# First gate products moved into the opening, down products turned, a third PSUM bank

## The chip, the core and the metric

The kernel runs on one core of a Trainium2 chip. The metric is the device time of one execution in microseconds. Five engines have a part in it: TensorE (PE in the rows, its weight loads PEld), VectorE (DVE), ScalarE (ACT), GpSimd (POOL), and SyncE (SP), which here only issues DMAs and waits.

## The reference

A recurrence over 768 steps for 4 batches and 8 heads of width 48, then a gated layer over its 3072 rows of 384 numbers:

```python
for t in range(S):                       # S = 768
    cur = np.einsum('bhd,bhe->bhde', u[None] * kt, vt)
    y[:, :, t] = np.einsum('bhd,bhde->bhe', rt, state + cur)
    state = wt[:, :, :, None] * state + np.einsum('bhd,bhe->bhde', kt, vt)
...
gate = 1.0 / (1.0 + np.exp(-(x @ w_gate)))   # 384 -> 1536
val = x @ w_val                              # 384 -> 1536
return (gate * val @ w_out).astype(np.float32)   # 1536 -> 384
```

The weights come as 64-bit numbers. The kernel unpacks each into a high and a low part of 32 bits, and forms each product of the gated layer from three matmuls: low part by high, high by low, high by high.

## The kernel before, in words

The recurrence is cut into 6 pieces of 128 steps. With 4 batches this makes 24 chunks of attention, q = 0 to 23, of which four (one for each batch) make up a row n = q // 4 of the gated layer, 512 tokens. A chunk q turns its keys (`turn_k`, tile pk), forms scores and sums (`pairs`, `add_up`, tiles pa and pv), mixes (`mix`) and turns its result (`turn_x`, tile px). Each of these tiles is a PSUM bank from `att_bank` (L204), which has two in turn.

The gated layer of a row n runs over 12 slices f of the hidden width. A slice is: `gate` (L480, nine matmuls into bank pg, through `up`), `sigmoid` on ACT, `value` (L487, nine matmuls into bank pu), `hidden` on DVE (the product, L492), `hidden_hi` on ACT (hh, L496), `hidden_lo` on DVE (hl, L500), and `down` (L502), which adds into the banks po0 to po3, one for each 128 tokens: there the tokens' hidden numbers are the stationary operand and 384 columns of the weights move. With the last slice `down` also copies each of the four banks by ACT (L515) into a tile o of a pool with two buffers, and issues its way out from ACT's queue (L517).

PSUM has eight banks: two of `att_bank`, pg, pu, po0 to po3.

The order is written in two ways. The opening (rows n = 0 and 1 of the gated layer in four groups of two batches, the attention's chunks 0 to 11, the unpacking of all weights, and the beginnings of chunks 12 and 13) is put in order by `Plan` (L142): `add` gives each step an engine, a cost, what it comes after, a rank, and the banks or buffers that it takes or gives back; `run` starts on each engine the step of lowest rank that is ready. Behind it comes the late loop (L630), written out by hand: for n from 2 to 5 and twelve slices each, the gate products of a slice, a part of the attention's chunk for row n + 1, the value products, another part, and then the down products of the slice before, which stand in `last`. In the row n = 5 no attention is left. The engines take their instructions in the order in which they are listed.

At the end every engine loads a flag and branches around `general` (L651), a slow way for inputs out of bounds, which does not run here.

Of the kernel before, what the change touches and what calls it, by code (L numbers as in the profile page):

```python
# [44 lines left out]
def general(ctx: ExitStack, tc: tile.TileContext, dec, tok, wts, u, out, whi, wlo, ident):  # L45
# [5 lines left out]
    rows = ctx.enter_context(tc.tile_pool(name="rows", bufs=1, space=bass.MemoryType.DRAM)).tile([B, S, DM], F32, name="rows")  # L51

    def tiles(name, shape, dtype=F32):
        return pool.tile(shape, dtype, name=name)
# [36 lines left out]
    for c in range(NC_):  # L91
        for b in range(B):
            nc.sync.dma_start(d[:, b], dec[b * NC_ + c])
        with tc.For_i(0, C) as i:
            def at(first, step):
                return d[:, :, first:first + NP * step].rearrange("a b (p c) -> a b p c", c=step)[:, :, :, bass.ds(i, 1)].broadcast_to(shape)
            for o in range(2):
                for b in range(B):
                    nc.sync.dma_start(vb[64 * o:64 * o + D, b], values[c, 2, o, bass.ds(i, 1), b].partition_broadcast(D))
            nc.vector.tensor_tensor(out=kv, in0=vb, in1=at(WW, C), op=ALU.mult)  # L100
            nc.vector.tensor_tensor(out=mix, in0=kv, in1=ub, op=ALU.mult)
            nc.vector.tensor_tensor(out=mix, in0=mix, in1=state, op=ALU.add)
            nc.vector.tensor_tensor(out=mix, in0=mix, in1=at(WW + NP * C, C), op=ALU.mult)
            nc.vector.tensor_tensor(out=state, in0=state, in1=at(1, W1), op=ALU.mult)
            nc.vector.tensor_tensor(out=state, in0=state, in1=kv, op=ALU.add)
            for j in range(2):
                nc.tensor.matmul(py[j][:2, :DM], lhsT=heads, rhs=mix[:, 2 * j:2 * j + 2], start=True, stop=True)
                nc.scalar.copy(y[:, 2 * j:2 * j + 2], py[j][:2, :DM].rearrange("a (b p e) -> a b p e", b=2, e=D))
            for b in range(B):
                for o in range(2):  # L110
                    nc.sync.dma_start(
                        rows[b, bass.ds(c * C + i, 1)].rearrange("t (p o e) -> o t p e", o=2, e=D)[o], y[o:o + 1, b])
# [5 lines left out]
    flat = rows.rearrange("b s e -> (b s) e")  # L118
    with tc.For_i(0, NG) as g:
        nc.sync.dma_start(x, flat[bass.ds(g * C, C)])  # L120
        for k in range(NKT):
            nc.tensor.transpose(out=px[:, k * C:(k + 1) * C], in_=x[:, k * P:(k + 1) * P], identity=ident)
        px3 = px[:, :DM].rearrange("a (k c) -> a k c", c=C)
        nc.scalar.copy(xhi, px3)
        nc.vector.tensor_tensor(out=xlo, in0=px3, in1=xhi.bitcast(F32), op=ALU.subtract)
        for f in range(NFF):
            for s, acc in enumerate((pg, pu)):
                for k in range(NKT):
                    cols = slice(s * DM + k * P, s * DM + (k + 1) * P)
                    for j, (w, a) in enumerate(((wlo, xhi), (whi, xlo), (whi, xhi))):  # L130
                        nc.tensor.matmul(acc[:, :C], lhsT=w[f][:, cols], rhs=a[:, k], start=k == 0 and j == 0, stop=k == NKT - 1 and j == 2)
            nc.scalar.activation(gate, pg[:, :C], AF.Sigmoid)
# [3 lines left out]
            for j, (a, w) in enumerate(((hl, whi), (hh, wlo), (hh, whi))):  # L136
                nc.tensor.matmul(po[:, :DM], lhsT=a, rhs=w[f][:, 2 * DM:], start=f == 0 and j == 0, stop=f == NFF - 1 and j == 2)
        nc.scalar.copy(x, po[:, :DM])
        nc.sync.dma_start(out[bass.ds(g * C, C)], x)


class Plan:  # L142
# [49 lines left out]
def tile_kernel(ctx: ExitStack, tc: tile.TileContext, dec: bass.AP, tok: bass.AP, wts: bass.AP, u: bass.AP, out: bass.AP):  # L192
# [5 lines left out]
    p2 = own.enter_context(tc.tile_pool(name="p2", bufs=2))  # L198
    ps1 = own.enter_context(tc.tile_pool(name="ps1", bufs=1, space=PSUM))
    att2 = own.enter_context(tc.tile_pool(name="att2", bufs=2, space=PSUM))  # L200
    early = tc.tile_pool(name="early", bufs=4)
    stage = early.__enter__()

    def att_bank(name):  # L204
        return att2.tile([P, 512], F32, tag="att", name=name)

    ident = const.tile([P, P], F32, name="ident")
# [33 lines left out]
        return raws[f].bitcast(dtype).rearrange("a (c w) -> a c w", w=2)[:, :, i]  # L241

    def w_guard(f):
        sq = p1.tile([P, 3 * DM], F32, tag="sq", name=f"sq{f}")
        nc.scalar.activation(sq, word(f, 1, F32), AF.Square, accum_out=acc_s[:, f:f + 1])
        nc.scalar.activation(sq, sq, AF.Relu, bias=1.0, scale=-1.0 / TINY ** 2, accum_out=acc_t[:, f:f + 1])

# [24 lines left out]
    def place(q):  # L272
        return q % B * NC_ + q // B
# [228 lines left out]
    def down(n, f, i0, i1):  # L502
        hh, hl = hid["hi", n, f, i0], hid["lo", n, f, i0]
        for i in range(i0, i1):
            if f == 0:
                po[n, i] = ps1.tile([P, 512], F32, tag=f"po{i}", name=f"po{n}_{i}")
            c = slice((i - i0) * C, (i - i0 + 1) * C)
            for j, (h, w) in enumerate(((hl, whi), (hh, wlo), (hh, whi))):
                nc.tensor.matmul(  # L509
                    po[n, i][:, :DM], lhsT=h[:, c], rhs=w[f][:, 2 * DM:],  # L510
                    start=f == 0 and j == 0, stop=f == NFF - 1 and j == 2,
                )
            if f == NFF - 1:
                o = p2.tile([P, DM], F32, tag="o", name=f"o{n}_{i}")
                nc.scalar.copy(o, po[n, i][:, :DM])  # L515
                g = place(n * B + i)
                nc.scalar.dma_start(out[g * C:(g + 1) * C, :], o)  # L517

    def check_bounds():
        nc.vector.tensor_scalar(out=fine[:L, 0], in0=acc_d, scalar1=2.0 ** 90, scalar2=None, op0=ALU.is_le)  # L520
# [14 lines left out]
    def add(name, engine, cost, after, rank, f=None, *args, take=(), give=()):  # L535
        plan.add(name, engine, cost, after, rank, f and (lambda: f(*args)), take, give)
# [46 lines left out]
    for g, (n, i0, i1) in enumerate(GROUPS):  # L583
        m = i1 - i0
        for f in range(NFF):
            a, name = (n, f, i0, i1), f"{g}_{f}"
            k = 100 + f + LAGS[g]
            soon = k / 1000 - 1
            up_cost = 9 * (0.008 + 0.056 * m)
            need = [f"xl{n * B + i}" for i in range(i0, i1)] + [f"wl{f}", f and f"pu{g}_{f - 1}"]  # L590
            add("pg" + name, "PE", up_cost, need, k, gate, *a, take=["pg", "unit"] + [f"po{i}" for i in range(i0, i1) if f == 0])
            add("sg" + name, "ACT", 0.14 + 0.13 * m, ["pg" + name], soon, sigmoid, *a, give=["pg"])
            add("pu" + name, "PE", up_cost, ["pg" + name], k, value, *a, take=["pu"])
            add("hm" + name, "DVE", 0.15 + 0.135 * m, ["pu" + name, "sg" + name], soon, hidden, *a, give=["pu"])
# [12 lines left out]
    def steps(q):  # L607

# [75 lines left out]
```

## Time and profile before

| what | us |
|---|---|
| median of three runs | 605.04 (603.53 to 608.01) |
| profiled execution, its own time | 603.9 |
| its span, from the first to the last instruction | 602.2 |
| PE busy | 558.7 |
| DVE busy | 332.6 |
| ACT busy | 201.6 |
| POOL busy | 96.7 |

The time of an execution is that of the device; the span is what the profiler saw of it, 1.7 us less. Busy times overlap, so they say which engine is full, and not where the time goes. In a timeline the first column is the start in us from the span's start, the second the duration; matmuls follow each other faster than they last, so that the pace of a run of matmuls is read from the starts of two groups. A matmul's end is modelled. A bracket at the end of a row is the idle time ahead of it and what ended it.

### The profile page before, as it was taken

The page shows a single profiled execution, that of the slowest core. Times are in us where ns is not written, and L with a number is a line of the kernel's source. Part 1 is how long each engine was busy: PE and PEld are TensorE (multiplying, and loading weights), DVE is VectorE, ACT ScalarE, POOL GpSimd, SP SyncE. Part 2 cuts the span into 40 slices and gives each one's busy share as a digit, 9 for nine tenths or more (in the row PEclk, how much of TensorE's full clock was granted, in tenths as well). Part 3 has the DMA queues.
Part 4 walks back from the last instruction along what each step waited for, and adds up shares of the span by engine and source line. Part 5 has one row for each costly group of instructions (what it writes and reads, how often), then busy time and mean ns, then how long its engine had stood idle before and what let it go on. Part 6 is the DMA issues. An engine that isn't in the chain of part 4 may idle for free. (4 is left out here: it accounts for less than half of the span.)

```text
span 602.2 us, 14593 instructions
## 1 busy us (share of the span) xinstructions
PE 558.7 (93%) x6474; PEld 498.4 (83%) x6474; DVE 332.6 (55%) x570; ACT 201.6 (33%) x402; POOL 96.7 (16%) x86
## 2 busy tenths in 40 slices
PE   4475899999999999899999999999999999999994
PEld 3365799999999999788888888888888888888883
DVE  4989879989685653254554554554454453221220
ACT  3648683444333322312222322222321221222212
POOL 3352111102120502002201211211211210000000
PEclk9999699999999999999999999999999999999997
DMA  8788920033233130122033033022033000100001
GB/s 250 250 327 290 347 95 1 1 87 83 72 121 126 50 125 3 53 86 86 3 87 87 28 112 86 2 86 87 35 106 87 1 1 2 54 1 0 1 1 57
DMA packets 12055, 50.85 MB, mean 84 GB/s; under 512 B 1376, under 2 KB 4576, under 8 KB 10448
## 3 DMA queue, kind: packets, MB, share of 16 engines
q1 hardware_dynamic: 8528, 45.11, 23.4%
q10 hardware_dynamic: 3456, 4.72, 2.2%
q8 instruction: 53, 0.87, 0.6%
q14 instruction: 18, 0.15, 0.1%
HBM read 45.11 MB, written 4.72 MB: 83 GB/s over the span
## 5 line engine op out<-in xcount | busy, mean ns | idle before, releaser
L474 PE MATMUL pg<-x,w 128*128 128x256 f32 (+1 forms) x864 | 171.6, 344 | 2.1 <-DVE w L267 2.1
L474 PE MATMUL pu<-x,w 128*128 128x256 f32 (+1 forms) x864 | 170.5, 342 | 0.0
L474 PEld LDWEIGHTS pg<-x,w 128*128 128x128 f32 x864 | 138.3, 193 | 17.8 <-DVE w L267 2.2
L474 PEld LDWEIGHTS pu<-x,w 128*128 128x128 f32 x864 | 136.2, 191 | 17.3
L509 PE MATMUL po<-w,hh 128*128 128x384 f32 x576 | 147.7, 337 | 0.0
L492 DVE TENSOR_TENSOR sg<-pu,sg 128x256 f32<-128x256 f32 (+1 forms) x96 | 53.4, 557 | 149.9 <-PE pu L474 148.9
L509 PE MATMUL po<-w,hl 128*128 128x384 f32 x288 | 101.2, 351 | 7.1 <-DVE hl L500 7.0
L496 ACT CAST hh<-sg 128x256 fp32r<-128x256 f32 (+1 forms) x96 | 49.2, 512 | 170.0 <-DVE sg L492 169.6
L509 PEld LDWEIGHTS po<-w,hh 128*128 128x128 f32 x576 | 105.0, 189 | 0.9
L485 ACT ACTIVATE sg<-pg 128x256 f32<-128x256 f32 (+1 forms) x96 | 46.9, 488 | 141.7 <-PE pg L474 140.1
L314 POOL TENSOR_TENSOR bon<-tok,a 128x384 f32<-128x384 f32 x24 | 35.0, 1457 | 282.7 <-DVE a L310 282.7
L500 DVE TENSOR_TENSOR hl<-sg,hh 128x256 fp32r<-128x256 f32 (+1 forms) x96 | 55.7, 580 | 39.0 <-ACT hh L496 39.0
L509 PEld LDWEIGHTS po<-w,hl 128*128 128x128 f32 x288 | 54.3, 189 | 10.4 <-DVE hl L500 8.4
L303 POOL TENSOR_TENSOR bon<-tok,ub 128x384 f32<-128x384 f32 x24 | 32.6, 1358 | 113.4 <-DMA tok<-tok 61.1
L448 DVE TENSOR_TENSOR bon<-pa,bon 128x192 f32<-128x192 f32 x48 | 15.6, 353 | 49.3 <-PE pa L441 49.2
L348 ACT ACTIVATE junk<-eg 112x1032 bf16<-112x1032 f32 x24 | 25.6, 1066 | 30.7 <-DVE eg L338 30.6
L321 DVE TENSOR_TENSOR_SCAN eg<-pin,ends 112x516 f32<-112x516 f32 x24 | 30.0, 1251 | 4.9 <-DMA pin<-dec 4.9
L338 DVE TENSOR_TENSOR_SCAN eg<-pin,heads 112x516 f32<-112x516 f32 x24 | 30.5, 1270 | 0.0
L353 PE MATMUL pk<-ident,pin 112*128 112x112 f32 x96 | 14.7, 278 | 14.1 <-DVE pin L327 10.2
L306 POOL TENSOR_TENSOR bon<-bon,tok 128x384 f32<-128x384 f32 x24 | 27.3, 1136 | 1.7
L441 PE MATMUL pa<-tok,at 64*32 64x48 f32 x1536 | 23.8, 213 | 2.3 <-DVE at L402 2.3
L353 PEld LDWEIGHTS pk<-ident,pin 112*128 112x128 f32 x96 | 11.5, 150 | 17.1 <-issue 9.0
(62 smaller groups left out, 433.8 us busy)
## 6 DMA issues: line engine op xcount, KB each, us to landing
pin<-dec SPq DMA_DIRECT2D x23, 675.5 KB, 5.8
tok<-tok SPq DMA_DIRECT2D x24, 576.0 KB, 5.8
wraw<-wts SPq DMA_DIRECT2D x12, 1152.0 KB, 12.3
y<-o ACTq DMA_DIRECT2D x24, 192.0 KB, 1.9
pin<-dec SPq DMA_DIRECT2D x1, 448.0 KB, 4.3
pin<-dec SPq DMA_DIRECT2D x1, 227.5 KB, 2.9
ub<-u SPq DMA_DIRECT2D x1, 192.0 KB, 6.7
```

Source lines behind the costliest of these rows:

```text
L303: nc.gpsimd.tensor_tensor(out=bon[q], in0=tk[q][:, 0:DM], in1=ub, op=ALU.mult)
L306: nc.gpsimd.tensor_tensor(out=bon[q], in0=bon[q], in1=tk[q][:, DM:2 * DM], op=ALU.mult)
L314: nc.gpsimd.tensor_tensor(out=by_head(bon[q]), in0=by_head(tk[q][:, 2 * DM:]), in1=a0, op=ALU.mult)
L321: nc.vector.tensor_tensor_scan(out=e[:, 516:0:-1], data0=t[:, 516:0:-1], data1=ends[:, 516:0:-1], initial=0.0, op0=ALU.mult, op1=ALU.add,)
L338: nc.vector.tensor_tensor_scan(out=e[:, WW:WW + 516], data0=t[:, 0:516], data1=heads[:, 0:516], initial=0.0, op0=ALU.mult, op1=ALU.add,)
L353: nc.tensor.transpose(out=t[:, p * L:(p + 1) * L], in_=kk(q)[:, p], identity=ident[:L, :L])
L474: nc.tensor.matmul(t, lhsT=w[f][:, cols], rhs=x[n][:, a, k, i0 * C:i1 * C], start=k == 0 and j == 0, stop=k == NKT - 1 and j == 2)
L485: nc.scalar.activation(sg, hid["g", n, f, i0], AF.Sigmoid)
L492: nc.vector.tensor_tensor(out=sg, in0=hid["u", n, f, i0], in1=sg, op=ALU.mult)
L496: nc.scalar.copy(hh, hid["s", n, f, i0])
L500: nc.vector.tensor_tensor(out=hl, in0=hid["s", n, f, i0], in1=hid["hi", n, f, i0].bitcast(F32), op=ALU.subtract)
L509: nc.tensor.matmul(po[n, i][:, :DM], lhsT=h[:, c], rhs=w[f][:, 2 * DM:], start=f == 0 and j == 0, stop=f == NFF - 1 and j == 2,)
```

## The change

Five things change. The lines of the changed kernel stand some 20 to 43 lines further down than those of the kernel before.

The nine gate products of the late loop's first slice (n = 2, f = 0) become a step of the opening's plan, with the highest rank number, after the gate products of the last two groups; the late loop leaves them out.

For n from 2 to 5 `down_turned` takes the place of `down`: the weights are the stationary operand, and all 512 tokens' hidden numbers move, so that each of three banks po0 to po2 holds 128 outputs of 512 tokens. Each bank is copied into a buffer of its own; in the last row the second block is copied by DVE and sent by SyncE. The output is written turned for these rows, in blocks, and the host turns it back.

The bank po3, which these rows do not need, is the third one of `att_bank` in the late loop.

The tile sq, which receives the squares of the weights' guard, is bf16 instead of fp32. `general` writes the same blocks; it is written out for each block of rows instead of looping.

```diff
     def att_bank(name):
+
+        turns.append(name)
+        if late and len(turns) % 3 == 0:
+            return ps1.tile([P, 512], F32, tag="po3", name=name)
         return att2.tile([P, 512], F32, tag="att", name=name)
...
-        sq = p1.tile([P, 3 * DM], F32, tag="sq", name=f"sq{f}")
+        sq = p1.tile([P, 3 * DM], BF16, tag="sq", name=f"sq{f}")
...
                 nc.scalar.copy(o, po[n, i][:, :DM])
-                g = place(n * B + i)
-                nc.scalar.dma_start(out[g * C:(g + 1) * C, :], o)
+                nc.scalar.dma_start(out[n].rearrange("(b c e) -> b c e", b=B, c=C)[i], o)
+
+    def down_turned(n, f, i0, i1):
+
+        hh, hl = hid["hi", n, f, i0], hid["lo", n, f, i0]
+        for k in range(NKT):
+            if f == 0:
+                po[n, k] = ps1.tile([P, 512], F32, tag=f"po{k}", name=f"po{n}_{k}")
+            cols = slice(2 * DM + k * P, 2 * DM + (k + 1) * P)
+            for j, (h, w) in enumerate(((hl, whi), (hh, wlo), (hh, whi))):
+                nc.tensor.matmul(po[n, k], lhsT=w[f][:, cols], rhs=h, start=f == 0 and j == 0, stop=f == NFF - 1 and j == 2)
+            if f == NFF - 1:
+                o = p1.tile([P, B * C], F32, tag=f"ot{k}", name=f"o{n}_{k}")
+                y = po[n, k]
+                by_vector = n == NC_ - 1 and k == 1
+                if by_vector:
+                    nc.vector.tensor_copy(out=o, in_=y)
+                else:
+                    nc.scalar.copy(o, y)
+                to = out[n].rearrange("(k p t) -> k p t", p=P, t=B * C)[k]
+                (nc.sync if by_vector else nc.scalar).dma_start(to, o)
...
+    ahead = (2, 0, 0, B)
+    add("ahead", "PE", 2.1, [f"xl{2 * B + i}" for i in range(B)] + ["pg2_11", "pg3_11"], 200, gate, *ahead, take=["pg"])
...
     plan.run()
     early.__exit__(None, None, None)
     stage = own.enter_context(tc.tile_pool(name="late", bufs=2))
+    late = True
...
                 a = (n, 3 * j + i, 0, B)
-                gate(*a)
+                if a != ahead:
+                    gate(*a)
                 sigmoid(*a)
...
                 if last:
-                    down(*last.pop())
+                    down_turned(*last.pop())
...
-    down(*last.pop())
+    down_turned(*last.pop())
```

Where the opening ends, PE had the last group's value products (pu_2_11, slice 11 of the group that starts at the third batch), its down products into po_2 and po_3, and then the late loop's first gate products (pg_0_0):

```order
L474 MATMUL pu_2_11_3325<-x_1106,w_1682 128x256 x9
L509 MATMUL po_2_2326<-w_1682,hl_2_11_3338 128x384
L509 MATMUL po_2_2326<-w_1682,hh_2_11_3336 128x384 x2
L509 MATMUL po_3_2330<-w_1682,hl_2_11_3338 128x384
L509 MATMUL po_3_2330<-w_1682,hh_2_11_3336 128x384 x2
L474 MATMUL pg_0_0_3356<-x_2412,w_236 128x512 x9
L353 MATMUL pk_3368<-ident,pin_2819 128x112 x4
L474 MATMUL pu_0_0_3375<-x_2412,w_236 128x512 x9
```

In the changed kernel the same place on PE reads:

```order
L494 MATMUL pu_2_11_3325<-x_1106,w_1682 128x256 x9
L494 MATMUL pg_0_0_3335<-x_2412,w_236 128x512 x9
L529 MATMUL po_2_2326<-w_1682,hl_2_11_3348 128x384
L529 MATMUL po_2_2326<-w_1682,hh_2_11_3346 128x384 x2
L529 MATMUL po_3_2330<-w_1682,hl_2_11_3348 128x384
L529 MATMUL po_3_2330<-w_1682,hh_2_11_3346 128x384 x2
L373 MATMUL pk_3368<-ident,pin_2819 128x112 x4
L494 MATMUL pu_0_0_3375<-x_2412,w_236 128x512 x9
```

The gate products have moved ahead of the six down products, and nothing else here has moved.

At the program's end, ACT had the last hh, four copies of the banks po_0 to po_3 with an issue behind each, and the flag:

```order
L496 CAST hh_0_11_6680<-sg_0_11_6667 128x512
L515 COPY o_0_6699<-po_0_6290 128x384
L517 DMA y<-o_0_6699 128x384
L515 COPY o_1_6705<-po_1_6294 128x384
L517 DMA y<-o_1_6705 128x384
L515 COPY o_2_6711<-po_2_6298 128x384
L517 DMA y<-o_2_6711 128x384
L515 COPY o_3_6717<-po_3_6302 128x384
L517 DMA y<-o_3_6717 128x384
L651 TENSOR_LOAD flag
L651 COMPARE_AND_BRANCH
```

In the changed kernel ACT's end is:

```order
L516 CAST hh_0_11_6529<-sg_0_11_6516 128x512
L554 COPY o_0_6545<-po_0_6170 128x512
L556 DMA y<-o_0_6545 128x512
L554 COPY o_2_6557<-po_2_6178 128x512
L556 DMA y<-o_2_6557 128x512
L694 TENSOR_LOAD flag
L694 COMPARE_AND_BRANCH
```

Two copies and two issues are left on ACT; the block between them has gone to DVE and SyncE. SyncE's end in the changed kernel, behind the last loads of the attention's inputs (pin, tok):

```order
L301 DMA pin_5607<-dec 112x1544
L306 DMA tok_5609<-tok 128x1152
L556 DMA y<-o_1_6551 128x512
L694 TENSOR_LOAD flag
L694 COMPARE_AND_BRANCH
```

Before, the flag's load stood right behind the last load of tok there; now the issue of an output block stands between.

## Rows read from the trace of the kernel before

**Rows 1.** The page: span, and busy time, share of the span and instructions.

```profile
span 602.2 us, 14593 instructions
PE 558.7 (93%) x6474; PEld 498.4 (83%) x6474; DVE 332.6 (55%) x570; ACT 201.6 (33%) x402; POOL 96.7 (16%) x86
```

**Rows 2.** Table of stretches: from:to, length, busy of each engine, PEclk, DMA share, GB/s.

```profile
270.00:330.00 60.00, 60.00 (x738) 51.44 (x738) 29.46 (x53) 15.59 (x31) 12.41 (x9) 1.00 0.22 63
```

**Rows 3.** Waits of PE, 270 us to the end: total, times, longest (us).

```profile
PE total L527 <- DVE count L525: 0.7, 1, 0.7
```

**Rows 4.** Timeline of PE, the end of the opening.

```profile
245.07 1.23 PE L474 MATMUL pu<-x,w 128*128 128x256 f32 x9
247.77 0.44 PE L509 MATMUL po<-w,hl 128*128 128x384 f32 x1 [1.48 <-DVE hl L500]
...
248.95 2.25 PE L474 MATMUL pg<-x,w 128*128 128x512 f32 x9
251.03 0.55 PE L353 MATMUL pk<-ident,pin 112*128 112x112 f32 x4
```

**Rows 5.** Timeline of ACT, the sigmoid of the opening's last gate.

```profile
243.31 0.38 ACT L485 ACTIVATE sg<-pg 128x256 f32<-128x256 f32 x1
```

**Rows 6.** Timeline of PE, the late loop: its first value products, and slices of the last row.

```profile
251.35 2.30 PE L474 MATMUL pu<-x,w 128*128 128x512 f32 x9
253.59 0.69 PE L370 MATMUL pa<-pin 48*64 48x64 f32 x32
...
537.26 2.20 PE L474 MATMUL pu<-x,w 128*128 128x512 f32 x9
539.30 0.33 PE L509 MATMUL po<-w,hl 128*128 128x384 f32 x1
...
541.41 2.24 PE L474 MATMUL pg<-x,w 128*128 128x512 f32 x9
```

**Rows 7.** Timeline of ACT, the end of the program.

```profile
592.34 0.48 ACT L515 COPY o<-po 128x384 f32<-128x384 f32 x1 [1.61 <-PE po L509]
592.85 0.34 ACTq L517 DMA_DIRECT2D y<-o  x1
...
593.79 1.03 ACTq L517 DMA_DIRECT2D y<-o  x1
595.92 0.48 ACT L515 COPY o<-po 128x384 f32<-128x384 f32 x1 [2.16 <-SPq L651]
...
597.38 0.64 ACTq L517 DMA_DIRECT2D y<-o  x1
```

**Rows 8.** Timeline of PE, matmuls of the last slice's first and last down products.

```profile
591.79 0.51 PE L509 MATMUL po<-w,hh 128*128 128x384 f32 x2
...
593.35 0.51 PE L509 MATMUL po<-w,hh 128*128 128x384 f32 x2
```

**Rows 9.** The flag's line, L651: duration ns min/median/max, first and last start us.

```profile
L651 SPq EVENT_SEMAPHORE  x8: 17/17/17, 526.4 to 599.7; - x8
L651 SPq TENSOR_LOAD <-flag x1: 572/572/572, 522.9 to 522.9; - x1
...
L651 SPq COMPARE_BRANCH  x1: 45/45/45, 523.6 to 523.6; - x1
...
L651 ACTq COMPARE_BRANCH  x1: 54/54/54, 598.6 to 598.6; - x1
L651 ACTq EVENT_SEMAPHORE  x1: 17/17/17, 601.3 to 601.3; - x1
```

**Rows 10.** Groups by form: count | busy us, mean ns of one | idle before, releasers.

```profile
L492 DVE TENSOR_TENSOR sg<-pu,sg 128x512 f32<-128x512 f32 x48 | 33.2, 692 | 119.9 <-PE pu L474 119.9
...
L485 ACT ACTIVATE sg<-pg 128x512 f32<-128x512 f32 x48 | 28.5, 593 | 104.2 <-PE pg L474 103.4 <-PE pa L380 0.8
L348 ACT ACTIVATE junk<-eg 112x1032 bf16<-112x1032 f32 x24 | 25.6, 1066 | 30.7 <-DVE eg L338 30.6
...
L246 ACT ACTIVATE sq<-sq 128x1152 f32<-128x1152 f32 x12 | 14.0, 1166 | 0.4
```

More of the change, by code (lines that the diff above doesn't have):

```diff
@@ L50, in general @@
     bank = ctx.enter_context(tc.tile_pool(name="banks", bufs=1, space=PSUM))
-    rows = ctx.enter_context(tc.tile_pool(name="rows", bufs=1, space=bass.MemoryType.DRAM)).tile([B, S, DM], F32, name="rows")
+    rows = ctx.enter_context(tc.tile_pool(name="rows", bufs=1, space=bass.MemoryType.DRAM)).tile([NC_, B, C, DM], F32, name="rows")
     def tiles(name, shape, dtype=F32):
@@ L111, in general @@
                     nc.sync.dma_start(
-                        rows[b, bass.ds(c * C + i, 1)].rearrange("t (p o e) -> o t p e", o=2, e=D)[o], y[o:o + 1, b])
+                        rows[c, b, bass.ds(i, 1)].rearrange("t (p o e) -> o t p e", o=2, e=D)[o], y[o:o + 1, b])
     x, px = tiles("x", [P, DM]), bank.tile([P, 512], F32, name="px")
@@ L117, in general, with feed @@
     pg, pu, po = (bank.tile([P, 512], F32, name=n) for n in ("pg", "pu", "po"))
-    flat = rows.rearrange("b s e -> (b s) e")
-    with tc.For_i(0, NG) as g:
-        nc.sync.dma_start(x, flat[bass.ds(g * C, C)])
+    def feed(n, b, turned):
+        nc.sync.dma_start(x, rows[n, b])
         for k in range(NKT):
@@ L135, in general @@
             nc.vector.tensor_tensor(out=hl, in0=h, in1=hh.bitcast(F32), op=ALU.subtract)
-            for j, (a, w) in enumerate(((hl, whi), (hh, wlo), (hh, whi))):
-                nc.tensor.matmul(po[:, :DM], lhsT=a, rhs=w[f][:, 2 * DM:], start=f == 0 and j == 0, stop=f == NFF - 1 and j == 2)
-        nc.scalar.copy(x, po[:, :DM])
-        nc.sync.dma_start(out[bass.ds(g * C, C)], x)
+            for k in range(NKT if turned else 1):
+                cols = slice(2 * DM + k * P, 2 * DM + (k + 1) * P)
+                for j, (a, w) in enumerate(((hl, whi), (hh, wlo), (hh, whi))):
+                    first, done = f == 0 and j == 0 and k == 0, f == NFF - 1 and j == 2
+                    if turned:
+                        nc.tensor.matmul(po[:, k * C:(k + 1) * C], lhsT=w[f][:, cols], rhs=a, start=first, stop=done, skip_group_check=True)
+                    else:
+                        nc.tensor.matmul(po[:, :DM], lhsT=a, rhs=w[f][:, 2 * DM:], start=first, stop=done)
+        nc.scalar.copy(x, po[:, :DM])
+        if turned:
+            to = out[n].rearrange("(k p b c) -> b p k c", p=P, b=B, c=C)[b]
+            nc.sync.dma_start(to, x.rearrange("p (k c) -> p k c", c=C))
+        else:
+            nc.sync.dma_start(out[n].rearrange("(b c e) -> b c e", b=B, c=C)[b], x)
+    for n in range(NC_):
+        for b in range(B):
+            feed(n, b, n >= 2)
 class Plan:
@@ L200, in tile_kernel @@
     att2 = own.enter_context(tc.tile_pool(name="att2", bufs=2, space=PSUM))
+    late = False
     early = tc.tile_pool(name="early", bufs=4)
     stage = early.__enter__()
+    turns = []
     def att_bank(name):
+        turns.append(name)
+        if late and len(turns) % 3 == 0:
+            return ps1.tile([P, 512], F32, tag="po3", name=name)
         return att2.tile([P, 512], F32, tag="att", name=name)
@@ L515, in down @@
                 nc.scalar.copy(o, po[n, i][:, :DM])
-                g = place(n * B + i)
-                nc.scalar.dma_start(out[g * C:(g + 1) * C, :], o)
+                nc.scalar.dma_start(out[n].rearrange("(b c e) -> b c e", b=B, c=C)[i], o)
[4 more added lines that the diff above has]
+                po[n, k] = ps1.tile([P, 512], F32, tag=f"po{k}", name=f"po{n}_{k}")
+            cols = slice(2 * DM + k * P, 2 * DM + (k + 1) * P)
+            for j, (h, w) in enumerate(((hl, whi), (hh, wlo), (hh, whi))):
[6 more added lines that the diff above has]
+                    nc.vector.tensor_copy(out=o, in_=y)
+                else:
+                    nc.scalar.copy(o, y)
+                to = out[n].rearrange("(k p t) -> k p t", p=P, t=B * C)[k]
+                (nc.sync if by_vector else nc.scalar).dma_start(to, o)
     def check_bounds():
@@ L678 @@
     args = [nc.dram_tensor(n, a.shape, mybir.dt.from_np(a.dtype), kind="ExternalInput").ap() for n, a in arrays.items()]
-    args.append(nc.dram_tensor("y", (B * S, DM), F32, kind="ExternalOutput").ap())
+    args.append(nc.dram_tensor("y", (NC_, B * C * DM), F32, kind="ExternalOutput").ap())
     with tile.TileContext(nc) as tc:
@@ L682 @@
     r = run_bass_kernel_spmd(nc, [arrays], core_ids=[0])
-    return r.results[0]["y"]
+    y = r.results[0]["y"]
+    y = np.concatenate([y[:2].reshape(-1, B * C, DM), y[2:].reshape(-1, DM, B * C).transpose(0, 2, 1)])
+    return np.ascontiguousarray(y.reshape(NC_, B, C, DM).transpose(1, 0, 2, 3).reshape(B * S, DM))
```

## The prediction

> **What bounds the kernel now.** I read four views: the page's busy times and the table of stretches (which engine is full, where), the list of TensorE's waits (whom it waits for), then the timeline at the three places that the diff touches, and last the rows of the program's end.
>
> TensorE (PE) is busy for 558.7 of a span of 602.2 us [rows 1]. In the table of stretches the reader is to see 60.00 us busy of 60.00 from 270 to 330, at a granted clock of 1.00, its upper level of 2.4 GHz [rows 2]; the three next stretches up to 510 read alike. From 270 us to the end the list of PE's waits has one row, 0.7 us [rows 3]. So up to about 250 us, while the attention and the unpacking of weights run beside the products, PE sometimes waits; behind that it is the bound, and only fewer or shorter PE instructions, or a shorter end, give time back. A wait taken from ACT, VectorE (DVE) or a queue there is worth nothing.
>
> **The change part by part.** The profiled execution took 603.9 us, span 602.2; the median of the three runs is 605.04. I work out what is saved and take it from all three alike.
>
> *The gate products of the late loop's first chunk, nine matmuls of 512 columns, are listed ahead of the opening's last down products.* Before, PE ends the opening's last value products (issued at 245.07, 1.23 long, so to 246.3), waits 1.48 us for hl of DVE, starts six down products at 247.77, is at the gate products at 248.95 and through their issue at 251.03 [rows 4]. Six down products so cost 1.18 and nine gate products 2.08. Now the gate products start at some 246.2 (the next matmul may be issued about 0.1 before the modelled end of the last) and end at 248.3. By then hl has been there for 0.5 us, so the down products begin at once. Their first matmul no longer stands behind a wait, so they take some 1.05 to 1.1, and PE is at the next work at 249.3 to 249.4 instead of 251.03: **1.7 us**. The gate products' only wait is for ACT's read of their bank, which was at 243.31, 0.38 long [rows 5]. What was late next, ACT's sigmoid of this gate, stays behind the opening's two last output copies, but those come at PE's pace too. Bounds: 1.48, the wait alone, to 1.8.
>
> *Down products of n from 2 to 5 turned.* Each of 48 chunks had 12 matmuls of 384 columns (3 for each of 4 blocks of rows) and now has 9 of 512 (3 for each of 3 blocks of outputs): 4608 columns either way, 1.92 us at 2.4 GHz. The trace has both shapes side by side: in the last stretch, where no attention runs beside, twelve down products from 539.30 to 541.41, 2.11 us; nine value products of the same 512 columns, with a weight slice as the stationary operand as the turned ones have it, from 537.26 to 539.30, 2.04 us [rows 6]. Over the bare columns this is 15.8 ns for each matmul of 384 and 13.3 for each of 512. Three matmuls fewer at 13.3 to 15.8 ns are 0.040 to 0.047 us; the plain difference is 0.07, of which the rest may be due to what DVE and ACT do beside. I take 0.045. It counts in 46 chunks: the last one starts when hl comes, whichever shape is ahead of it, and one chunk is followed by PE's wait for the bounds' count [rows 3], which swallows it. 46 x 0.045 = **2.1 us**. The trace shows no turned product with hl or hh as moving operand, so the bounds are wide: at best 0.07 x 46 = 3.2; at worst the slowest nine products of 512 columns that these rows show, from 251.35 to 253.59, 2.24 us [rows 6], which would be 0.13 x 46 = 6.0 lost. I stay at the value products, whose form is the nearest.
>
> The Trainium skill, "TensorE: Matmul & The Clock Gate", section "Back-to-back issue gap", gives N / 2.4 + 2.5 ns for a warm matmul of N columns; the rows show a fixed part of 13.3 to 15.8 ns, so they do not agree. By the Trainium skill's figure the 138 matmuls fewer (3 x 46) would be worth an estimated 0.35 us in place of 2.1.
>
> *The end.* Before, the program's last four output copies share two buffers. The reader is to see that ACT copies and sends two, and starts the third only at 595.92 after an idle of 2.16 [rows 7], though the last matmul pair, 0.51 long, starts at 593.35 [rows 8]. The row names SyncE as the releaser, but the code has the reason: the third copy takes the first one's buffer, which must have landed. The last issue starts at 597.38, takes 0.64, and 4.2 us later the span ends. In these 4.2 ACT loads the flag, branches at 598.6 and has its next instruction at 601.3 [rows 9]: 2.7 us for nothing but the branch, then 0.9 of closing. Now three blocks have three buffers, and nothing waits for a landing. PE ends at 593.86 as before, since the last hl sets that. ACT's copy started 0.04 behind its last matmul (591.79 + 0.51, then 592.34 [rows 7, 8]), so the last one starts at 593.9. It has 512 columns from PSUM, 0.59 us as the sigmoid of this shape [rows 10]: 594.5. Its issue takes 0.34 to 1.03, as the rows have it [rows 7], so it ends at 594.9 to 595.5; and 4.2 us more give 599.1 to 599.7, 2.5 to 3.1 less than 602.2. A second path is new: the block that DVE copies (0.69 [rows 10], to about 593.9) goes out by SyncE, which before had branched at 523.6 and now issues at 594.0, 0.3 long, loads the flag (0.57), branches and stands for 2.8 us (523.6 to 526.4 [rows 9]): 597.7. I allow 1 us for its eight waits [rows 9] and what follows them, which before lay beside ACT's branch, and the closing 0.9: 599.6. So I take **2.7 us**, bounds 1.0 to 3.2.
>
> The Trainium skill, "Runtime: NRT & Kernel Launch", section "Instruction fetch mechanics", says that a taken branch to a page that is not loaded must fetch it first. The 2.7 and 2.8 us agree, and it is a reason to expect them once more on each engine that now branches late.
>
> *What costs or gives nothing.* The third bank for the attention's chunks: it can only take waits away, and PE has none behind 270 us [rows 3]; where the attention's results come from ACT or DVE, one or two products of over 2 us lie between. Cover gone, a bank's wait would be one copy, 0.6 us. The guard's squares in bf16: ACT took 1166 ns for 1152 fp32 outputs and 1066 for 1032 bf16 outputs [rows 10], 1.01 and 1.03 ns each, so the type hardly matters to ACT; 0.02 ns more for 1152 outputs in 24 passes would be 0.55 us, the bound either way, and it would mostly lie beside DVE's work on the same weights. Outputs in blocks: the same bytes, three issues instead of four, 0.6 us of copy instead of 0.48, on an ACT that mostly waits for PE.
>
> Sum: 1.7 + 2.1 + 2.7 = 6.5 us. Span 602.2 to 595.7, profiled execution 603.9 to 597.4, median 605.04 to **598.5**.
>
> **Rivals.**
>
> *The end moves less.* SyncE's and DVE's late branches, each with its own fetch, and two transfers of 256 KB that land together, take the place of the removed buffer wait. For it: ACT's issues took 0.64 and 1.03 where others took 0.34 [rows 7], so the end is crowded already. Against it: the 2.16 us of idle are really gone. With 1.0 instead of 2.7: 600.2.
>
> *Columns alone count.* If the 0.07 comes not from the number of matmuls but from what lies beside them, the turned products take the 2.11 of the others, and turning gives nothing: 1.7 + 2.7 = 4.4, 600.6. For it: the two shapes stand in other parts of a chunk, with other work of DVE and ACT beside them. Against it: the rows are from chunks without any attention beside them [rows 6], and the difference is there. By the Trainium skill's 2.5 ns (the page and section above) it would be an estimated 600.3, and the rows do not bear that figure out.
>
> *More than I take.* Turned products at the full pace of the value products, 3.2, and the end at 3.1: 1.7 + 3.2 + 3.1 = 8.0, 597.0.
>
> *Slower.* The turned product is no value product: its moving operand was written by DVE and ACT one chunk ago, and the other buffers of the same pool are written meanwhile. If its nine take 2.24 us, 6.0 are lost against 4.4 won at both ends: 606.6. It decides from 2.11 + 4.4 / 46 = 2.21 us for nine, 245 ns each; slower by over 1% needs some 260 ns each. For it only the slow nine behind the transposes [rows 6]; against it every other nine.
>
> *The change does not do what it says*: the gate moved but held by something I do not see. Then 1.7 is missing, 600.2; I count it within my own case's range.
>
> **How the numbers follow.** My case 0.64, 597.0 to 600.2; the end moves less 0.12; columns alone 0.10; more than I take 0.09; slower 0.05. About 1% is what a measurement of this kernel can tell from no change; for faster that is 599.0 or less. Of my case some two thirds lie there (0.42), with all of the fourth and a little of the others: faster 0.52. Slower by over 1% is left for the turned products alone, 0.03; the rest is 0.45. The range takes in the two cases near 600.4 with the spread of the runs (603.5 to 608.0): 596.3 to 602.5.
>
> **What would show it.** Right: no wait of 1.48 before the opening's last down products, and the gate products right behind the value products; the turned nine at 2.04 to 2.08 us, each chunk 0.04 to 0.05 shorter; the last output copy 0.04 behind the last matmul, and the span's end 5.2 to 5.9 us behind that copy's start. Wrong: turned products over 235 ns apart, new waits of PE behind 250 us, or SyncE's branch as the last thing before the closing by over 1 us.

## The result and the profile after

The changed kernel took 596.59 us (median of four, 595.38 to 597.80), the kernel before 605.28 in the same comparison: a ratio of 0.9853, 95% interval [0.9826, 0.988], so 1.5% faster where 1.1% was forecast. Six further times gave 597.35 against 605.16, ratio 0.986 [0.9837, 0.9883]. The profiled execution took 595.38 against 603.9, with this span and these busy times on its page [rows 1]:

```profile
span 593.7 us, 14287 instructions
PE 555.1 (93%) x6330; PEld 478.6 (81%) x6330; DVE 332.6 (56%) x571; ACT 200.2 (34%) x397; POOL 96.4 (16%) x86
```

The instruction counts fall by 144 matmuls and 144 weight loads, three for each of 48 slices. The span is 8.5 us shorter. To find where, I cut both traces at the same four points. The first three are in PE's timeline of the changed kernel: the start of the opening's last value products (244.15), of the late loop's first transposes (248.35), and of the down products of the last slice but one (582.84) [rows 4]:

```profile
244.15 1.23 PE L494 MATMUL pu<-x,w 128*128 128x256 f32 x9
245.22 2.23 PE L494 MATMUL pg<-x,w 128*128 128x512 f32 x9
247.28 0.33 PE L529 MATMUL po<-w,hl 128*128 128x384 f32 x1
...
248.35 0.55 PE L373 MATMUL pk<-ident,pin 112*128 112x112 f32 x4
...
582.84 0.39 PE L546 MATMUL po<-hl,w 128*128 128x512 f32 x1
...
586.96 0.61 PE L546 MATMUL po<-hh,w 128*128 128x512 f32 x2
```

The kernel before has 245.07 and 251.03 at the first two points [rows 4] and 589.11 at the third, by its timeline of PE:

```profile
589.11 0.33 PE L509 MATMUL po<-w,hl 128*128 128x384 f32 x1
```

The fourth point is the end of the last matmul: 593.35 + 0.51 before [rows 8], 586.96 + 0.61 after. The last column of the table is the saving that was forecast.

| stretch, us | before | after | saved | forecast |
|---|---|---|---|---|
| start to the opening's last value products | 245.07 | 244.15 | 0.9 | 0 |
| from there to the first pk | 5.96 | 4.20 | 1.8 | 1.7 |
| from there to the last slice but one's down products | 338.08 | 334.49 | 3.6 | 2.1 |
| from there to the end of the last matmul | 4.75 | 4.73 | 0.0 | 0 |
| from there to the span's end | 8.3 | 6.1 | 2.2 | 2.7 |

The reader sees in the rows why the second stretch shrank: the 1.48 of waiting ahead of the down products is gone, and the gate products stand in its place. In the list of PE's waits from 270 us on, the count's row [rows 3] is still there, and hl's at the last slice is new, with 0.2 us:

```profile
PE total L566 <- DVE count L564: 0.9, 1, 0.9
PE po L546 <- DVE hl L520: 0.2, 1, 0.2
```

The third stretch shows itself in two slices of the last row, where no attention runs. The starts of the groups in PE's timeline are 2.04 us apart, for down, gate and value alike:

```profile
533.88 0.39 PE L546 MATMUL po<-hl,w 128*128 128x512 f32 x1
...
535.92 2.20 PE L494 MATMUL pg<-x,w 128*128 128x512 f32 x9
537.96 2.20 PE L494 MATMUL pu<-x,w 128*128 128x512 f32 x9
540.00 0.39 PE L546 MATMUL po<-hl,w 128*128 128x512 f32 x1
```

Before they were 2.11 (down) and 2.04 (value) apart [rows 6], and the gate products behind the down products took 2.08, from this row of the timeline of before to the value products at 537.26 [rows 6]:

```profile
535.18 2.24 PE L474 MATMUL pg<-x,w 128*128 128x512 f32 x9
```

Where the attention stands right ahead of the down products, these gain less: in a slice with `turn_x` ahead of them they took 2.19 us before (the first two rows) and 2.17 after, from start to start:

```profile
260.93 0.42 PE L509 MATMUL po<-w,hl 128*128 128x384 f32 x1
...
263.12 2.24 PE L474 MATMUL pg<-x,w 128*128 128x512 f32 x9
```

```profile
258.27 0.48 PE L546 MATMUL po<-hl,w 128*128 128x512 f32 x1
...
260.44 2.21 PE L494 MATMUL pg<-x,w 128*128 128x512 f32 x9
```

Added up from such starts over the whole stretch, the down products took 1.9 us less than before, the gate products 1.8 less, and the value products 0.1 more.

At the end, ACT's timeline has no idle time for a buffer any more [rows 7], and the rows of the flag's line show SyncE, DVE and ACT branching within 1.7 us of each other; before, SyncE had branched 75 us ahead of ACT [rows 9]:

```profile
586.24 0.59 ACT L554 COPY o<-po 128x512 f32<-128x512 f32 x1 [1.78 <-PE po L546]
...
587.61 0.59 ACT L554 COPY o<-po 128x512 f32<-128x512 f32 x1 [0.78 <-PE po L546]
588.23 0.36 ACTq L556 DMA_DIRECT2D y<-o  x1
```

```profile
L694 SPq EVENT_SEMAPHORE  x8: 17/17/17, 591.7 to 592.3; - x8
...
L694 DVEq COMPARE_BRANCH  x1: 72/72/72, 587.6 to 587.6; - x1
...
L694 SPq COMPARE_BRANCH  x1: 45/45/45, 588.6 to 588.6; - x1
...
L694 ACTq COMPARE_BRANCH  x1: 54/54/54, 589.3 to 589.3; - x1
...
L694 ACTq EVENT_SEMAPHORE  x1: 17/17/17, 592.4 to 592.4; - x1
```

Between branch and next instruction lie 3.1 us, on SyncE as on ACT, where the kernel before had 2.8 and 2.7. Both are ready at nearly the same time, and 1.3 us behind ACT's 592.4 the span ends.

### The profile page after: what moved, and what is told of

The parts are those of the page before. It is cut to its first block, busy times and chain, and to the rows that moved or that the text cites. A ratio compares the mean times of both kernels' runs of the same rounds, so it can differ in the third digit from the quotient of the medians.

```text
span 593.7 us, 14287 instructions
## 1 busy us (share of the span) xinstructions
PE 555.1 (93%) x6330; PEld 478.6 (81%) x6330; DVE 332.6 (56%) x571; ACT 200.2 (34%) x397; POOL 96.4 (16%) x86
## 4 chain that ended last, share of the span: by engine, by line
PE 86%; DVE 7%; DMA 3%; issue 1%; ACT 1%; SPq 0%; ACTq 0%; DVEq 0%
PE pu L494 25%; PE pg L494 25%; PE po L546 16%; PE po L529 8%; PE pa L461 3%; PE pa L390 2%; PE pa L400 2%; DMA wraw<-wts 2%; PE pk L373 1%; PE px L473 1%; PE pv L437 1%; DVE eg L341 1%; DMA pin<-dec 1%; PE pa L437 1%; DVE full L275 1%
## 5 line engine op out<-in xcount | busy, mean ns | idle before, releaser
L494 PE MATMUL pg<-x,w 128*128 128x256 f32 (+1 forms) x864 | 169.0, 341 | 1.2 <-DVE w L287 1.2
L546 PE MATMUL po<-hh,w 128*128 128x512 f32 x288 | 89.1, 390 | 0.0
L546 PEld LDWEIGHTS po<-hh,w 128*128 128x128 f32 x288 | 54.1, 188 | 10.8
L546 PE MATMUL po<-hl,w 128*128 128x512 f32 x144 | 58.7, 407 | 0.2 <-DVE hl L520 0.2
L529 PE MATMUL po<-w,hh 128*128 128x384 f32 x192 | 49.7, 340 | 0.0
L529 PE MATMUL po<-w,hl 128*128 128x384 f32 x96 | 34.5, 359 | 6.0 <-DVE hl L520 6.0
L529 PEld LDWEIGHTS po<-w,hh 128*128 128x128 f32 x192 | 35.5, 192 | 0.0
L546 PEld LDWEIGHTS po<-hl,w 128*128 128x128 f32 x144 | 27.0, 188 | 6.2 <-DVE hl L520 0.6
```

What stands on the lines that cost most here:

```text
L494: nc.tensor.matmul(t, lhsT=w[f][:, cols], rhs=x[n][:, a, k, i0 * C:i1 * C], start=k == 0 and j == 0, stop=k == NKT - 1 and j == 2)
L529: nc.tensor.matmul(po[n, i][:, :DM], lhsT=h[:, c], rhs=w[f][:, 2 * DM:], start=f == 0 and j == 0, stop=f == NFF - 1 and j == 2,)
L546: nc.tensor.matmul(po[n, k], lhsT=w[f][:, cols], rhs=h, start=f == 0 and j == 0, stop=f == NFF - 1 and j == 2)
```

## The experiments

Two questions were open: what made the late loop 1.5 us faster than the forecast, and whether each part of the change gives what its stretch says. The stretches named are those of the table.

**The gate products back in their place.** The changed kernel without the plan's step:

```diff
...
-    add("ahead", "PE", 2.1, ...
...
-                if a != ahead:
-                    gate(*a)
+                gate(*a)
```

> The changed kernel with the late loop's first gate products back behind the opening's last down products. Theory (the moved gate fills the wait): the wait of some 1.5 us before those down products is back, and PE comes to the late loop's first transposes (pk) 1.7 to 1.8 us later after the opening's last value products: 5.9 to 6.0 us instead of 4.2. The pace of the late loop and the end do not change. Rival (the gain came from elsewhere in the opening, and something else would be late next): the distance changes by under 0.8 us.

Measured: 598.33 us, ratio 0.9876 [0.9835, 0.9918]. PE's timeline:

```profile
247.08 1.23 PE L494 MATMUL pu<-x,w 128*128 128x256 f32 x9
249.79 0.44 PE L529 MATMUL po<-w,hl 128*128 128x384 f32 x1 [1.48 <-DVE hl L520]
...
253.03 0.55 PE L373 MATMUL pk<-ident,pin 112*128 112x112 f32 x4
```

The wait of 1.48 is back to the digit, and the second stretch is 5.95 instead of 4.20. The late loop's stretch is 334.5, as in the changed kernel. So the moved gate is worth 1.75 us (4.20 instead of 5.95), and nothing in the late loop became late for it.

**Down products by rows again.** The kernel before with the moved gate, bf16 squares and buffers of its own for the outputs:

```diff
...
-                o = p2.tile([P, DM], F32, tag="o", name=f"o{n}_{i}")
-                nc.scalar.copy(o, po[n, i][:, :DM])
+                o = p1.tile([P, DM], F32, tag=f"o{i}", name=f"o{n}_{i}")
+                by_vector = n == NC_ - 1 and i == 2
+                if by_vector:
+                    nc.vector.tensor_copy(out=o, in_=po[n, i][:, :DM])
+                else:
+                    nc.scalar.copy(o, po[n, i][:, :DM])
...
-                nc.scalar.dma_start(out[g * C:(g + 1) * C, :], o)
+                (nc.sync if by_vector else nc.scalar).dma_start(out[g * C:(g + 1) * C, :], o)
...
```

> The kernel before with the moved gate, the squares in bf16, and four output buffers of their own (in the last row the third block by VectorE and SyncE), but with the down products of all rows as before: twelve of 384 columns, two banks for the attention. In the row without attention a slice took 6.23 us before and 6.12 in the changed kernel: down 2.106 against 2.040, gate behind it 2.081 against 2.043. Theory A (the run of 384-column matmuls slows what comes behind it): both are as before, 2.10 to 2.11 and 2.08, and from the first pk to the last slice's down products it takes 338.0 us again, 3.6 more than in the changed kernel. Theory B (the gate became faster by another placement of tiles or by the bf16 squares): down 2.10 to 2.11, gate 2.04, 1.8 us more than in the changed kernel. The end: within 0.5 us of the changed kernel's.

Measured: 601.74 us, ratio 0.9947 [0.9922, 0.9972]. PE's timeline in the row without attention:

```profile
530.36 2.24 PE L474 MATMUL pg<-x,w 128*128 128x512 f32 x9
532.44 2.20 PE L474 MATMUL pu<-x,w 128*128 128x512 f32 x9
534.48 0.33 PE L509 MATMUL po<-w,hl 128*128 128x384 f32 x1
...
536.59 2.24 PE L474 MATMUL pg<-x,w 128*128 128x512 f32 x9
```

Gate 2.08, value 2.04, down 2.11: all as before, and the late loop's stretch is 338.1. Theory A stands: the gate products are slow because of what is ahead of them, and turning gives 3.6 us in all. The span ends 6.1 us behind the last matmul here, with four blocks by rows and four buffers; so the end's gain comes from the buffers and the second queue, not from the turned shape. No run has the one without the other.

**Two banks for the attention.** The changed kernel with `att_bank` as before:

```diff
-        if late and len(turns) % 3 == 0:
-            return ps1.tile([P, 512], F32, tag="po3", name=name)
```

> The changed kernel without the third bank for the attention's chunks in the late loop. Theory (no wait of PE was there to be taken away): the late loop takes the same within 0.3 us, PE has no new wait behind 250 us. Rival (the third bank gave a part of what the late loop gained beyond the forecast): 0.5 to 1.8 us more.

Measured: 598.47 us, ratio 0.988 [0.9847, 0.9913]; the late loop's stretch 334.4 against 334.5, PE's waits behind 250 us the same two rows. The third bank gives nothing, as no wait was there to be taken away.

**Two output buffers, all copies on ACT.** The changed kernel with:

```diff
-                o = p1.tile([P, B * C], F32, tag=f"ot{k}", name=f"o{n}_{k}")
+                o = p2.tile([P, B * C], F32, tag="ot", name=f"o{n}_{k}")
...
-                by_vector = n == NC_ - 1 and k == 1
+                by_vector = False
```

> The changed kernel with two shared buffers for the turned outputs instead of three, and all three copies and issues of the last row on ScalarE. Theory (the landing of the first block held the third copy): the third copy starts 2.5 to 3.2 us behind the first one's end instead of 0.8, and the span ends 7.0 to 8.0 us behind PE's last matmul, instead of 6.1. Rival (branches and their fetches set the end in any case): 6.0 to 6.4 us.

Measured: 598.84 us, ratio 0.9885 [0.9839, 0.993]. ACT's timeline at the end:

```profile
590.22 0.59 ACT L554 COPY o<-po 128x512 f32<-128x512 f32 x1 [1.78 <-PE po L546]
...
593.68 0.59 ACT L554 COPY o<-po 128x512 f32<-128x512 f32 x1 [1.83 <-PEq L694]
```

The third copy starts 2.87 us behind the first one's end, with an idle of 1.83, and the span ends 7.3 us behind the last matmul. The first theory's numbers hold. The row names PE's own branch as the releaser of the third copy; as in the kernel before [rows 7], what it needs by the code is the first one's buffer. With two shared buffers three blocks end at 7.3 us behind the last matmul and four at 8.3 and 8.5 (the kernel before, and with the down products between gate and value); with buffers of their own the ends lie between 6.0 and 6.8 in the nine profiles that have them, with three blocks or four. That the fourth block costs something only while copies wait for landings rests on this one profile, against a spread of 0.8 us.

**Twice as many matmuls for the same columns.** The changed kernel with each turned product in two halves:

```diff
-                nc.tensor.matmul(po[n, k], lhsT=w[f][:, cols], rhs=h, start=f == 0 and j == 0, stop=f == NFF - 1 and j == 2)
+                for s in range(2):
+                    part = slice(s * 2 * C, (s + 1) * 2 * C)
+                    nc.tensor.matmul(
+                        po[n, k][:, part], lhsT=w[f][:, cols], rhs=h[:, part],
+                        start=f == 0 and j == 0 and s == 0, stop=f == NFF - 1 and j == 2, skip_group_check=True)
```

> The changed kernel with each turned down product of 512 columns cut into two of 256 (eighteen matmuls and weight loads in a slice instead of nine, the same columns). Theory (each matmul has a fixed part of 13 ns beside its columns): a slice's down products take 2.04 + 9 x 0.0133 = 2.16 us, the opening's nine of 256 columns (1.08) say the same, and the late loop takes 46 x 0.12 = 5.5 us more, 340.0. Rival (columns alone count, and the difference of the two shapes came from what lies beside them): 2.04 to 2.06, under 1 us more.

Measured: 603.51 us, ratio 0.9971 [0.9948, 0.9994], 6 to 7 us over the changed kernel. PE's timeline:

```profile
532.73 0.40 PE L548 MATMUL po<-hl,w 128*128 128x256 f32 x2
...
534.88 2.23 PE L494 MATMUL pg<-x,w 128*128 128x512 f32 x9
536.95 2.20 PE L494 MATMUL pu<-x,w 128*128 128x512 f32 x9
538.99 0.40 PE L548 MATMUL po<-hl,w 128*128 128x256 f32 x2
```

Eighteen take 2.15 us, 119.4 ns each: nine more matmuls cost 0.11, 12 ns each. The late loop's stretch is 339.7, 5.2 more. Columns alone do not count. The gate products behind the run of 256 take 2.07, between the 2.04 behind 512 and the 2.08 behind 384.

**Down products between gate and value.** The kernel before with:

```diff
                 trio[i][0]()
+                if last:
+                    down(*last.pop())
                 value(*a)
...
-                if last:
-                    down(*last.pop())
```

> The kernel before with the late loop's down products (rows, twelve of 384 columns) listed between a slice's gate and value products instead of behind the value products. Theory A1 (nine products of 512 columns that come behind a run of 384-column matmuls go slower, whichever they are): in the last row the value products, now behind the down products, take 2.08 and the gate products 2.04. Theory A2 (it is the gate products' own: their weight slices, bank or place in the slice): gate 2.08, value 2.04.

Measured in a single execution: 629.49 us. PE's timeline:

```profile
561.23 2.20 PE L474 MATMUL pg<-x,w 128*128 128x512 f32 x9
563.63 0.44 PE L509 MATMUL po<-w,hl 128*128 128x384 f32 x1 [0.19 <-DVE hl L500]
...
565.82 2.24 PE L474 MATMUL pu<-x,w 128*128 128x512 f32 x9
567.90 2.20 PE L474 MATMUL pg<-x,w 128*128 128x512 f32 x9
...
572.49 2.24 PE L474 MATMUL pu<-x,w 128*128 128x512 f32 x9
```

Now the value products, which stand behind the run of 384, take 2.08 (565.82 to 567.90), and the pace of the gate products is back at 2.04: they are followed 2.40 later because the down products wait for hl. A1 holds: it is the place behind the run, not the product.

The run also teaches what the order before was good for. From the first pk to the end of the last matmul it takes 367.9 us instead of 342.8, 25.1 more. In the row without attention PE now waits for hl in every slice: 6.67 us from slice to slice (565.82 to 572.49, the next value products) instead of 6.23 (535.18 to 541.41 in the timeline of before), 4.9 us in eleven slices. Most of the rest lies where one row of the gated layer gives way to the next. There it takes 15.49, 13.43 and 12.33 us from one slice's value products to the next ones, where the kernel before took 9.13, 9.13 and 7.34: 15.7 us together. At each of the three PE waits once, for 3.45, 2.39 (at 447.20) and 2.84 us:

```profile
351.41 0.93 PE L380 MATMUL pa<-ready,pin 48*64 48x48 f32 x3 [3.45 <-DVE at L402]
...
538.53 0.19 PE L527 MATMUL total<-count,ones 128*1 128x1 f32 x2 [2.84 <-DVE count L525]
538.65 4.21 PE L474 MATMUL pg<-x,w 128*128 128x512 f32 x9
```

During the wait, or within 2.1 us behind it, the granted clock falls to its lower level of 1.2 GHz: the nine gate products of a slice take 4.21 us here instead of 2.20. The table of stretches has a mean granted clock of 0.79 and then 0.50 around the first wait, where the kernel before kept 2.4 GHz [rows 2]:

```profile
348.00:352.00 4.00, 0.45 (x2) 0.29 (x2) 1.89 (x5) 1.66 (x4) 0.00 (x0) 0.79 0.27 98
352.00:356.00 4.00, 3.99 (x99) 3.79 (x100) 0.62 (x2) 0.00 (x0) 0.00 (x0) 0.50 0.45 134
```

The waits account for about half of the 15.7 us, the clock for the other half (an estimate: half of the time that PE ran at the lower level). Why PE waits at these three places was not taken apart.

**Rows with 512 columns.** The second experiment's kernel, with 128 more columns of the weights in each down product of the late loop:

```diff
+            wide = P if n >= 2 else 0
...
-                    po[n, i][:, :DM], lhsT=h[:, c], rhs=w[f][:, 2 * DM:],
+                    po[n, i][:, :wide + DM], lhsT=h[:, c], rhs=w[f][:, 2 * DM - wide:],
...
```

> The kernel with the down products of all rows as before, the moved gate and own buffers, but with 512 moving columns for n from 2 to 5 instead of 384: 128 columns more of the weights move, whose sums are not used. Twelve matmuls of 512 columns, the tokens' hh and hl as stationary operand. Theory B1 (the width of 384 columns is what slows the gate products behind it): the twelve take 12 x 0.2267 = 2.72 us and the gate products behind them 2.04. Theory B2 (the stationary operand that DVE and ACT have just written, or the twelve changes of weights from another tile): the gate products still take 2.08.

Measured in a single execution: 628.71 us. PE's timeline:

```profile
533.03 0.39 PE L510 MATMUL po<-w,hl 128*128 128x512 f32 x1
...
535.75 2.20 PE L474 MATMUL pg<-x,w 128*128 128x512 f32 x9
537.79 2.20 PE L474 MATMUL pu<-x,w 128*128 128x512 f32 x9
539.83 0.39 PE L510 MATMUL po<-w,hl 128*128 128x512 f32 x1
```

Twelve take 2.72 us, 226.7 ns each, and the gate products behind them 2.04. So neither the tokens' hh and hl as stationary operand nor the number of weight changes slows what follows; the width of 384 does (B1).

**The high part first.** The changed kernel with another order of the three matmuls, everywhere:

```diff
-            for j, (h, w) in enumerate(((hl, whi), (hh, wlo), (hh, whi))):
+            for j, (h, w) in enumerate(((hh, wlo), (hh, whi), (hl, whi))):
```

> The changed kernel with the three matmuls of each down product in another order: the two with the high part hh first, the one with the low part hl last, in the opening and in the late loop. hh is there some 0.7 us before hl, so where PE waits for hl ahead of down products the wait should be shorter by that: at the opening's end 1.2 becomes 0.5, and in the last slice the wait for hl of 0.2 (0.36 between starts) goes. Theory: 1.0 us off these two places, and up to 2 us more from the three waits further ahead in the opening, if nothing else is late there. Rival (hh's wait takes its place in full): 0 to 0.3 us.

Measured: 595.41 us, ratio 0.9837 [0.98, 0.9874]. PE's timeline:

```profile
241.96 1.23 PE L494 MATMUL pg<-x,w 128*128 128x256 f32 x9
243.93 0.61 PE L529 MATMUL po<-w,hh 128*128 128x384 f32 x2 [0.75 <-ACT hh L516]
244.39 0.44 PE L529 MATMUL po<-w,hl 128*128 128x384 f32 x1
...
245.20 1.23 PE L494 MATMUL pu<-x,w 128*128 128x256 f32 x9
```

The wait became 0.75, but hl then came late for the third matmul too: from gate to value 3.24 us instead of 3.58. In the last slice the wait is gone: from 583.89, the last slice but one's first matmul, to the last matmul's end it takes 4.31 us instead of 4.73. Together 0.8 us, where 1.0 was expected; more ahead in the opening can't be told from its spread (below).

**Both once more, side by side.**

> The changed kernel once more, unchanged, for more times of it. By the parts measured so far (1.75 at the opening's end, 3.6 in the late loop, 2.2 behind the last matmul) it should be 7.5 us below the kernel before, near 597.7; if the first four times (median 596.59, 8.7 below) are typical, something in the opening is faster too, and its last value products start by 1 us or more earlier than the 245.07 of the kernel before in this run as well.

> The kernel with the high part's matmuls first, once more, beside the changed kernel on the same chip. By the two places where its trace differs (0.34 us at the opening's last gate products, 0.43 in the last slice) it should be 0.8 us below the changed kernel; if nothing of that reaches the end, 0 to 0.2.

Measured on one chip: the changed kernel 597.35 us, ratio to before 0.986 [0.9837, 0.9883]; with the high part first 596.14, ratio 0.9852 [0.9829, 0.9875]. The difference of 1.2 has the sign and about the size that the two places give, but the intervals overlap: a gain is shown in the trace, not in the times. Of the changed kernel the opening's last value products start at 246.72 this time, 1.65 later than in the kernel before:

```profile
246.72 1.23 PE L494 MATMUL pu<-x,w 128*128 128x256 f32 x9
```

So the changed kernel is not faster ahead of this point, as its first profile alone might have suggested.

## Why the prediction was right, and where its sizes were off

**The moved gate**: forecast 1.7, measured 1.75, shown by undoing it. Every step of the working held: gate products 2.06 long right behind the value products, hl there by then, down products without a first wait in 1.07.

**The turned products**: forecast 2.1, measured 3.6. The down products themselves gave 1.9. That this is near the forecast is in part luck. In the 22 slices where the value products stand right ahead of them they took 2.04, the full pace of the value products, and saved 0.066 and not 0.045: of the 0.07 that I saw and cut down for what may run beside, all belonged to the shape. In the 23 slices with attention right ahead they saved only 0.02 to 0.04. The term that was missing is one that I had put at nothing: the gate products behind a run of 384-column matmuls took 2.08 before and take 2.04 now, 0.04 in each slice, 1.8 us in all. The row was there, as the start of the next group but one; I had taken 2.08 for the gate products' own pace. The exchange of down and value products, and the rows with 512 columns, show that it belongs to the run of 384.

The Trainium skill's figure ("TensorE: Matmul & The Clock Gate", section "Back-to-back issue gap"), 2.5 ns beside a matmul's columns, which the page gives for a matmul by itself, does not hold for the streams here: halves cost 12 ns for each matmul added, and twelve matmuls of 512 columns ran at 226.7 ns each, 13.3 over their columns.

**The end**: forecast 2.7, measured 2.2 in this profile; behind the last matmul the changed kernel's second profile took 6.8 us instead of 6.1, so the gain is 1.5 to 2.2. From the last output copy's start to the span's end it takes 6.1 us, where 5.2 to 5.9 had been named as a sign of being right. The mis-sized terms are the branch, 3.1 us on SyncE and on ACT, instead of the 2.7 and 2.8 that I took over, and the closing, 1.3 us behind ACT's first instruction after it instead of 0.9. ACT's branch took 2.65 to 2.70 us in the three profiles in which no other engine branched within 5 us ahead of it (before, two buffers, down products between gate and value), and 2.7 to 3.6 in the nine in which SyncE branched 0.7 to 1.1 us ahead. The rival on the end (that late branches take the place of the buffer's wait) named the right mechanism, but of its price of 1.7 us only 0.5 to 1.2 was paid. The page of the Trainium skill "Runtime: NRT & Kernel Launch", section "Instruction fetch mechanics", says that a taken branch to a page that is not loaded has to wait for a fetch. The 2.9 us of DVE and the 3.1 of SyncE and ACT agree, though no run shows the fetch itself.

**What gives nothing**: the third bank, 0.1 us either way, shown by undoing it. The squares in bf16: ACT's second pass took 1166 ns a tile before [rows 10] and 1164 after; it was not undone alone.

**What remains**: 1.75 + 3.6 + 2.2 = 7.5 us, so 597.7; the ten times of the changed kernel have medians of 596.59 and 597.35. The profiled execution had 0.9 us more in its opening. In the ten profiles with the same order of work up to the opening's last value products these start between 244.15 and 248.21, so 0.9 is within the spread. The clock seems to have a part in this spread: from 50 to 80 us, where it stood at its lower level of 1.2 GHz for a part of the time, its mean grant was 0.83 in the changed kernel's first profile (244.15), 0.77 in its second (246.72) and 0.72 in the profiles of the third and fourth experiments (247.48 and 248.15). It is not all of it, as the second experiment's profile came to this point last (248.21) at 0.83. Nothing was tried on it.

The time thus came out near the case "more than I take" (597.0), close to the lower end of the range, but not for that case's reasons. The down products gave 1.9 and not 3.2, and the end 1.5 to 2.2 and not 3.1; the 1.8 of the gate products stands in none of the cases.

## What to carry to other kernels

Where the same columns can be moved in fewer, wider matmuls, by exchanging which operand stands and which moves, each matmul saved is worth its fixed part (12 to 13 ns here; 22 for each of the three saved in a slice without attention), and it pays to look at the pace of the groups behind as well, since a narrow run can cost its followers nearly as much as itself (1.8 against 1.9 us here). Where PE waits for an operand at the seam of two phases, listing independent products ahead of the wait gave its full length. Listing the down products one step too early, on the other hand, cost 25 us, most of it where rows meet. At a program's end, copies that share buffers wait for landings; buffers of their own and a second queue together gave 1.5 to 2.2 us, and late branches took a part back.

## What the runs showed of the hardware that I had not expected

Nine matmuls of 512 columns take 2.04 us behind nine or twelve others of 512, 2.07 behind eighteen of 256 and 2.08 behind twelve of 384, whichever product they are; the nine after these are at 2.04 again. The delay does not sit at the seam: behind 384 the nine start 224 to 236 ns apart, behind 512 they start 226 or 227 apart. Nine of 256 columns do not show it: in the opening they take 1.07 us behind a run of 384 and 1.08 behind others of 256. What causes it is open. A weight load is recorded as lasting 188 to 193 ns, longer than the 173 ns from one matmul of 384 to the next and shorter than the 227 of 512; but a run of 256, at 119 ns still further below it, slows the nine behind it less than one of 384, and no run took this apart.

With the down products a step too early, PE waited once for 2.4 to 3.5 us at each of three places, and during that wait or within 2.1 us behind it its clock was granted at the lower level, also while PE was busy again (3.99 of 4.00 us at 0.50, from 352 to 356). The short waits for hl in each slice of the last row did not do this: from 548 to 600 us the granted clock was 1.00.
